# DeltaNet with soft mixture of experts: expert weights loaded as half rows, with the ReLU restoring column order

## The chip, the cores and the metric

The kernel runs on one core of one Trainium2 chip. The metric is the device time of the whole program in microseconds. Before the change it is 296.39 us, the median of three runs (295.6 to 298.61).

## The reference

First comes a delta-rule attention over 768 steps, for 4 batches and 8 heads of 48 dimensions. Its output, as 3072 rows of 384 columns, is the input x of a soft mixture of 8 experts with 4 slots each.

```python
for t in range(S):                                  # S = 768
    y[:, :, t] = einsum('bhd,bhde->bhe', q[:, :, t], state)
    v_old = einsum('bhde,bhd->bhe', state, kt)      # kt is the normalised key
    state = state + bt * einsum('bhd,bhe->bhde', kt, vt - v_old)

logits = x @ phi                                    # 3072 x 32
d = softmax(logits, over the rows);  slot_input = d.T @ x
for e in range(8):
    h = maximum(slot_input[e] @ w1[e], 0.0)         # w1[e] is 384 x 1024
    slot_out[e] = h @ w2[e]                         # w2[e] is 1024 x 384
out = softmax(logits, over the slots) @ slot_out    # 3072 x 384
```

All is float32. Each w1 and w2 is 12.6 MB over the eight experts.

## The kernel before

The recurrence is cut into 12 chunks of 64 steps. For each chunk the kernel loads k, q and v (`load`, `load_q`; rows of 192 bytes), transposes them, forms the Gram matrices, inverts a triangular system (`invert`, `join`), and steps the state (`step`). As chunks finish, `route` and `pair` transpose the outputs, compute logits and accumulate the slot inputs. The mixture's tail then runs: a merge of partial sums, `first` (slot inputs times w1, ReLU, transposes), `second` (times w2), and the combination with its stores.

All work is recorded as operations of a `Plan`. Three tables written into the file fix everything afterwards: `ORDER` gives the order in which the operations are issued, `PLACE` the address of each buffer, and `ALTS` which engine takes an operation that several could do. So a loop in the source does not tell the order on an engine. Waits between engines and transfers are put in where the regions that two instructions touch overlap. SyncE (SP) and GpSimd (POOL) issue the weight loads, each among its other work. A transfer that SP issues also waits for the one eight places before it.

Weights. A w1 tile holds, for expert e and kk in 0..2, one row of 1024 columns on each of 128 partitions (partition p has row 3p + kk). It is loaded by two transfers: columns 0 to 511 into the first half of the tile, 512 to 1023 into the second. There are 24 such tiles, so 48 transfers of 256 KB: 32 issued by SP, 16 by POOL (L1029). A w2 tile holds, for expert e and tp in 0..3, two rows of 384 columns on each partition (t = 2 tp and 2 tp + 1). Each row is one transfer into its half of the tile. There are 32 such tiles, so 64 transfers of 192 KB: 46 by SP, 18 by POOL (L1040).

`first(qq)` takes four experts at a time (a quartet), side by side in the four row groups of one PSUM bank. For each half f of the hidden columns it accumulates three products per expert (L1090), then a ReLU with the expert's mask evicts the bank into the half f of `hr` (L1099, on ScalarE). Eight transposes (L1106) read `hr` with a stride of 8, so that they need both halves, and give `hT`. The order table runs the second quartet's products first.

`second` (L1123) runs twice, for the halves h of the 384 output columns. It loops over both quartets and over tp; each (quartet, tp) is a group of 8 matmuls: t even for four experts, then t odd for four experts. The columns that a matmul reads in a w2 tile start at `x = Dm * (t % 2) + HD * h`, with Dm = 384 and HD = 192. After each pass a copy (L1128), a product that sums the experts' rows (L1129) and a scaling (L1130) give the slots' outputs; the combination (L1142) and the stores follow (L1150: 48 transfers of 96 KB on SP, POOL and ScalarE). Matmuls in float32 stand as two instructions each in the profile.

Of the kernel before, what the change touches and what calls it, by code (L numbers as in the profile page):

```python
# [11 lines left out]
ALU = mybir.AluOpType  # L12
ACT = mybir.ActivationFunctionType
# [183 lines left out]
def kernel(  # L197
# [11 lines left out]
    nc = tc.nc  # L209
# [5 lines left out]
    E, Dm, F = moe_w1.shape  # L215
# [14 lines left out]
    def A(b, n=None):  # L230
        if b.psum:
            return pb[:, b.addr:b.addr + b.size, :]
        return sb[:, b.addr:b.addr + (n or b.size)]
# [40 lines left out]
    ENG = {"SP": nc.sync, "ACT": nc.scalar, "POOL": nc.gpsimd, "DVE": nc.vector}  # L274
# [11 lines left out]
    V = nc.vector  # L286
# [718 lines left out]
    for n in range(N):  # L1005
# [7 lines left out]
        for m in ([n - 1] if n else []) + ([n] if n == N - 1 else []):  # L1013
            route(m)
            if m % 2:
                pair(m // 2)

    w1b, w2b = {}, {}
    done = qslot + [kslot[x % NK] for x in (N - 1, *range(N - NK, N - 2))]
    last = [kslot[(N - 2) % NK]]  # L1020
    for e in range(E):
        for kk in range(NKT):
            w1b[e, kk] = t = done.pop(0) if done else pl.buf(F)
            pl.tag = ("w1", e)

            def go(q, e=e, kk=kk, t=t):
                s = moe_w1[e].rearrange("(p k) f -> p k f", k=NKT)
                for x in H2:
                    ENG[q].dma_start(out=A(t)[:, 512 * x:512 * x + 512], in_=s[:, kk, 512 * x:512 * x + 512])  # L1029
            pl.soft = [chain[8]]  # L1030
            pl.op(dq(0.8, 1.2, None), None, go, w=[t], bus=1.5, nd=2)
    for e in range(E):
        for tp in range(NFC // 2):
            w2b[e, tp] = t = last.pop() if last and e == E - 1 else pl.buf(2 * Dm)
            pl.tag = ("w2", e)

            def go(q, e=e, tp=tp, t=t):
                s = moe_w2[e].rearrange("(p t) d -> p t d", t=NFC)
                for x in H2:
                    ENG[q].dma_start(out=A(t)[:, Dm * x:Dm * x + Dm], in_=s[:, 2 * tp + x])  # L1040
            pl.soft = [chain[N - 1]]
            pl.op(dq(0.8, 1.2, None), None, go, w=[t], bus=1.15, nd=2)
    pl.soft = []
# [34 lines left out]
    HF = F // 2  # L1078

    def first(qq):  # L1080
        pl.tag = ("first", qq)
        hr = pl.buf(F)
        hTb[qq] = pl.buf(F)
        for f in H2:
            ph = pl.buf(1, psum=True)

            def prod(f=f, ph=ph):
                for kk in range(NKT):
                    for j in range(4):
                        mm(A(ph)[32 * j:32 * j + 32, 0], A(slb)[:, NSL * kk:NSL * kk + NSL],  # L1090
                           A(w1b[4 * qq + j, kk])[:, f * HF:f * HF + HF], start=kk == 0)
            pl.op("PE", 2.6, prod, r=[slb] + [w1b[4 * qq + j, kk] for j in range(4) for kk in range(NKT)], w=[ph], rec=24, act=3072)

            def relu(e, f=f, ph=ph):
                o = A(hr)[:, f * HF:f * HF + HF]
                if e == "DVE":
                    V.tensor_scalar(o, A(ph)[:, 0], 0.0, XMSK(qq), op0=ALU.max, op1=ALU.mult)
                else:
                    nc.scalar.activation(o, A(ph)[:, 0], ACT.Relu, scale=XMSK(qq))  # L1099
            pl.op([("ACT", 0.69), ("DVE", 0.75)], None, relu, r=[ph, cxm], w=[(hr, f)])  # L1100
        for t4 in H2:
            pt = pl.buf(1, psum=True)

            def turn4(t4=t4, pt=pt):
                for i in range(4):
                    nc.tensor.transpose(A(pt)[:, 0, P * i:P * i + P], A(hr)[:, 4 * t4 + i::NFC], ident())  # L1106
            pl.op("PE", 0.5, turn4, r=[hr, cident], w=[pt], rec=4, act=512)
            pl.op(ev(512), None, lambda e, t4=t4, pt=pt: copy(
                e, A(hTb[qq])[:, 512 * t4:512 * t4 + 512], A(pt)[:, 0]), r=[pt], w=[(hTb[qq], t4)])

    first(0)
    first(1)
    HD = Dm // 2
    for h in H2:
        pl.tag = ("second", h)
        pso = pl.buf(1, psum=True)
        for qq in H2:
            for tp in range(NFC // 2):
                def prod(tp=tp, qq=qq, h=h, pso=pso):
                    for t in (2 * tp, 2 * tp + 1):  # L1120
                        for j in range(4):
                            x = Dm * (t % 2) + HD * h
                            mm(A(pso)[32 * j:32 * j + 32, 0, 0:HD],  # L1123
                               A(hTb[qq])[:, P * t + 32 * j:P * t + 32 * j + 32],
                               A(w2b[4 * qq + j, tp])[:, x:x + HD], start=qq == 0 and t == 0)
                pl.op("PE", 0.76, prod, r=[(hTb[qq], tp // 2)] + [w2b[4 * qq + j, tp] for j in range(4)], w=[pso], rec=16, act=768)
        sj, so, p4 = pl.buf(HD), pl.buf(HD), pl.buf(1, psum=True)
        pl.op("ACT", t_act(HD), lambda sj=sj, pso=pso: nc.scalar.copy(A(sj), A(pso)[:, 0, 0:HD]), r=[pso], w=[sj])  # L1128
        pl.op("PE", 0.33, lambda p4=p4, sj=sj: mm(A(p4)[:, 0, 0:HD], A(csel4), A(sj)), r=[csel4, sj], w=[p4], rec=2, act=384)  # L1129
        pl.op("DVE", t_dvp(HD) + 0.05, lambda so=so, p4=p4: V.tensor_scalar(  # L1130
            A(so), A(p4)[:, 0, 0:HD], A(rd), None, op0=ALU.mult), r=[p4, rd], w=[so])
        pl.tag = ("out", h)
        for g2 in range(NG // 2):
            for z in H2:
                po, ob = pl.buf(2, psum=True), pl.buf(2 * Dm)

                def comb(po=po, z=z, g2=g2, so=so):
                    for x in H2:
                        for b in H2:
                            p0 = 32 * (2 * z + b)  # L1140
                            g = 2 * g2 + x
                            mm(A(po)[:, b, HD * x:HD * x + HD], A(cT)[p0:p0 + 32, P * g:P * g + P], A(so)[p0:p0 + 32])  # L1142
                pl.op("PE", 0.72, comb, r=[(cT, 2 * g2), (cT, 2 * g2 + 1), so], w=[po], rec=8, hold=[ob], act=384)
                pl.op(ev(2 * Dm), None, lambda e, po=po, ob=ob: copy(
                    e, A(ob).rearrange("p (b f) -> p b f", b=2), A(po)[:, :, 0:Dm]), r=[po], w=[ob])
                for b in H2:
                    def put(e, ob=ob, z=z, b=b, g2=g2, h=h):
                        o = out.rearrange("(y b g s t) d -> y b s t g d", y=2, b=2, g=NG, s=2)
                        for y in H2:
                            ENG[e].dma_start(out=o[y, b, z][:, 2 * g2:2 * g2 + 2, HD * h:HD * h + HD],  # L1150
                                             in_=A(ob)[ha(y), Dm * b:Dm * b + Dm].rearrange("p (x d) -> p x d", x=2))
                    pl.op(dq(0.85, 1.45, 0.95), None, put, r=[ob], bus=0.7, nd=2)
# [29 lines left out]
```

## Time and profile before

| what | value |
|---|---|
| median of the runs | 296.39 us |
| the profiled execution: time, span | 296.42 us, 294.7 us |
| granted TensorE clock, mean | 0.938 |
| TensorE busy (PE) | 228.9 us, 78% of the span |
| VectorE, ScalarE, GpSimd busy | 197.6, 145.2, 140.2 us |
| bytes moved | 45.13 MB, mean 153 GB/s |
| packets | 81519 in all, 74704 of them under 2 KB |

The span runs from the first to the last instruction; the profiled execution's own time has 1.7 us around it. PE is a TensorE matmul, PEld its weight load, DVE is VectorE, ACT is ScalarE. L12 is line 12 of the kernel before. A row of a group names line, engine, operation, output and input, count, busy time with the mean of one in ns, and the idle time before it with what ended it. A row of the windows has, for a stretch, the busy time and count of PE, PEld, DVE, ACT and POOL, then the granted clock, the busy share of the 16 DMA engines and GB/s. A row of transfers names the issuing queue (SPq is SP's), the count, the size of one and the median time from issue to landing; a row of a DMA queue has packets, MB and its share of the 16 engines (q1 carries what SP issues, q0 what POOL issues).

### The profile page before, as it was taken

Reading aid. Unit: us, or ns where it says so; the run is one execution under the profiler, and the core shown is the slowest. Engines: PE = TensorE matmul, PEld = TensorE weight load, DVE = VectorE, ACT = ScalarE, POOL = GpSimd, SP = SyncE. Lnnn points to the kernel's source line nnn. Section 1 sums busy time; section 2 is a strip of 40 time slices with the busy share of each in tenths; the row PEclk is TensorE's granted clock in tenths of the full one; section 3 lists DMA queues with packets and bytes.
Section 4 is the critical chain, followed back from the end, with each engine's and each line's share of the span. In section 5 each row is a group of like instructions: output and inputs, shape, how many; then the busy total and the mean of one; then the engine's idle time right before and its main releaser. Section 6 shows DMA issues by size and latency. Waiting matters only on the chain.

```text
span 294.7 us, 14440 instructions
## 1 busy us (share of the span) xinstructions
PE 228.9 (78%) x6252; PEld 186.2 (63%) x6252; DVE 197.6 (67%) x504; ACT 145.2 (49%) x325; POOL 140.2 (48%) x225
## 2 busy tenths in 40 slices
PE   0784778982988897798979877787866988999950
PEld 0663677872887786686868775766654864366640
DVE  3468979989866689777699889883773667213130
ACT  1253487774828466668736768562311532230321
POOL 8997569454493364226762545641640320200460
PEclk9997599999579999999899999999997999999985
DMA  8979642453431361336545407785696599990887
GB/s 147 162 155 166 111 79 56 97 107 56 87 56 34 73 118 33 62 54 136 116 94 118 153 4 232 215 190 177 200 349 218 178 349 375 349 364 13 213 226 206
DMA packets 81519, 45.13 MB, mean 153 GB/s; under 512 B 63520, under 2 KB 74704, under 8 KB 81456
## 3 DMA queue, kind: packets, MB, share of 16 engines
q1 hardware_dynamic: 72704, 30.28, 42.3%
q0 software_dynamic: 5232, 12.56, 15.0%
q10 hardware_dynamic: 3520, 1.38, 2.0%
q8 instruction: 49, 0.80, 1.1%
q14 instruction: 14, 0.11, 0.1%
HBM read 39.47 MB, written 4.72 MB: 150 GB/s over the span
## 4 chain that ended last, share of the span: by engine, by line
PE 27%; DVE 12%; issue 8%; SPq 4%; ACT 4%; POOL 2%; DMA 1%; DVEq 0%; POOLq 0%; ACTq 0%
SPq L1150 4%; DVE sb L277 4%; PE pb L1090 4%; PE pb L716 3%; PE pb L821 3%; ACT sb L281 2%; PE pb L1123 2%; PE pb L782 2%; PE pb L902 2%; PE pb L791 2%; POOL sb L277 2%; PE pb L504 2%; PE pb L867 1%; PE pb L920 1%; PE pb L953 1%
## 5 line engine op out<-in xcount | busy, mean ns | idle before, releaser
L281 ACT ACTIVATE sb<-pb 128x512 f32<-128x512 f32 (+5 forms) x144 | 76.0, 559 | 91.2 <-PE pb L473 22.9
L277 POOL TENSOR_TENSOR sb<-sb 128x256 f32<-128x256 f32 (+10 forms) x89 | 64.7, 735 | 66.8 <-DVE sb L277 33.5
L277 DVE TENSOR_TENSOR sb<-sb 128x126 f32<-128x126 f32 (+10 forms) x153 | 52.9, 347 | 11.2 <-POOL sb L277 6.7
L283 DVE COPY sb<-pb 128x512 f32<-128x512 f32 (+5 forms) x43 | 26.2, 617 | 27.3 <-PE pb L473 5.9
L473 PE MATMUL pb<-sb 128*128 128x128 f32 x192 | 32.7, 318 | 15.0 <-DMA sb<-in_q_dram 9.6
L473 PEld LDWEIGHTS pb<-sb 128*128 128x128 f32 x192 | 24.7, 161 | 19.4 <-issue 11.7
L716 PE MATMUL pb<-sb 64*64 64x32 f32 x1152 | 27.3, 231 | 11.9 <-DVE sb L277 4.7
L716 PEld LDWEIGHTS pb<-sb 64*64 64x64 f32 x1152 | 25.0, 147 | 15.2 <-issue 7.3
L504 PE MATMUL pb<-sb 64*64 64x128 f32 x768 | 28.2, 287 | 5.8 <-ACT sb L281 4.2
L840 PE MATMUL pb<-sb 64*64 64x48 f32 x768 | 26.2, 220 | 3.9 <-DVE sb L770 1.9
L840 PEld LDWEIGHTS pb<-sb 64*64 64x64 f32 x768 | 24.2, 135 | 6.6 <-DVE sb L770 2.5
L504 PEld LDWEIGHTS pb<-sb 64*64 64x64 f32 x768 | 22.7, 140 | 9.0 <-ACT sb L281 5.4
L782 PE MATMUL pb<-sb 64*64 64x48 f32 x768 | 26.0, 220 | 2.3 <-issue 2.3
L782 PEld LDWEIGHTS pb<-sb 64*64 64x64 f32 x768 | 24.1, 135 | 2.7 <-issue 2.5
L1040 POOL DMA_DIRECT2D sb<-in_moe_w_dram x18 | 9.7, 543 | 32.9 <-PE pb L953 16.1
L821 PE MATMUL pb<-sb 128*64 128x96 f32 x352 | 19.2, 260 | 3.2 <-ACT sb L281 1.6
L791 PE MATMUL pb<-sb 128*64 128x96 f32 x352 | 18.9, 261 | 1.9 <-ACT sb L513 0.8
L412 POOL DMA_DIRECT2D sb<-in_k_dram x35 | 19.7, 570 | 0.7 <-DVE sb L341 0.7
L821 PEld LDWEIGHTS pb<-sb 128*64 128x64 f32 x352 | 16.8, 145 | 4.9 <-ACT sb L281 2.2
L1150 POOL DMA_DIRECT2D out_dram<-sb x14 | 8.4, 607 | 23.8 <-DVE sb L283 18.5
L513 ACT ACTIVATE sb<-pb,sb 128x128 f32<-128x128 f32 x48 | 16.9, 368 | 4.9 <-PE pb L504 4.7
L791 PEld LDWEIGHTS pb<-sb 128*64 128x64 f32 x352 | 16.4, 145 | 3.6 <-issue 1.5
(142 smaller groups left out, 376.4 us busy)
## 6 DMA issues: line engine op xcount, KB each, us to landing
sb<-in_moe_w_dram SPq DMA_DIRECT2D x46, 192.0 KB, 5.5
sb<-in_moe_w_dram SPq DMA_DIRECT2D x32, 256.0 KB, 4.0
sb<-in_moe_w_dram POOLq DMA_DIRECT2D x16, 256.0 KB, 5.3
sb<-in_moe_w_dram POOLq DMA_DIRECT2D x18, 192.0 KB, 6.1
sb<-in_q_dram SPq DMA_DIRECT2D x14, 192.0 KB, 4.4
out_dram<-sb SPq DMA_DIRECT2D x24, 96.0 KB, 3.5
sb<-in_v_dram SPq DMA_DIRECT2D x22, 96.0 KB, 3.3
sb<-in_v_dram SPq DMA_DIRECT2D x88, 24.0 KB, 2.8
```

The costliest lines, as they stand in the source:

```text
L277: ENG[e].tensor_tensor(*a, **kw)
L281: nc.scalar.activation(o, i, ACT.Copy)
L283: V.tensor_copy(o, i)
L412: ENG[e].dma_start(out=d()[p0:p0 + w, x], in_=s[t0:t0 + w, hs])
L473: nc.tensor.transpose(A(ps)[:, 0, P * j:P * j + P], A(src)[:, x:x + P], ident())
L504: mm(A(ps)[ha(r), c, P * j4:P * j4 + P].rearrange("p (a t) -> p a t", a=2), x[ha(c), j, r, 0], x[ha(c), j, r])
L716: mm(A(ps)[ha(b), x, 64 * j:64 * j + RW].rearrange("p (a t) -> p a t", t=w), st, m)
L782: mm(pv(pY)[ha(1 - r), j // 4, j % 4, c], A(at)[ha(r), 512 * c + 64 * j:512 * c + 64 * j + 64], hv(u)[ha(r), j, c], start=first and c == 0 ...
L791: mm(A(pY)[ha(1 - r), j // 4, 96 * (j % 4):96 * (j % 4) + 96], kqv(KQ[n])[:, j, r, 1], Sv(n)[:, j, r], start=j % 4 == 0)
L821: mm(A(pR)[ha(r), j // 4, 96 * (j % 4):96 * (j % 4) + 96], kqv(KQ[n])[:, j, r, 0], Sv(n)[:, j, r])
L840: mm(pv(pW)[ha(r), j // 4, j % 4, c], A(zs)[ha(r), 64 * (zj * c + z0 + j):64 * (zj * c + z0 + j) + 64], hv(R)[ha(r), j, c])
L1150: ENG[e].dma_start(out=o[y, b, z][:, 2 * g2:2 * g2 + 2, HD * h:HD * h + HD], in_=A(ob)[ha(y), Dm * b:Dm * b + Dm].rearrange("p (x d) -> p ...
```

## The change

Each w1 transfer now takes, from every row, columns 256x to 256x + 255 and 512 + 256x to 512 + 256x + 255, for x = 0 or 1: two pieces of 1 KB in place of one of 2 KB. They fill half x of the tile. Each w2 transfer takes columns 192x to 192x + 191 of both rows t: two pieces of 768 B in place of one of 1536 B, again into half x of the tile.

`first` still reads half f of a w1 tile, but its 512 results are now hidden columns 256f and up and 512 + 256f and up, so that the ReLU writes them as two blocks of 256 that lie 512 apart and `hr` has the old order again. `second` reads its columns from `x = Dm * h + HD * (t % 2)`: pass h reads half h of each tile alone. The order of instructions on every engine, their number apart from a wait, the issuing queues and the buffers stay as they were.

```diff
--- before.py
+++ after.py
@@ -1015,6 +1015,7 @@
             if m % 2:
                 pair(m // 2)
 
+    HD = Dm // 2
     w1b, w2b = {}, {}
     done = qslot + [kslot[x % NK] for x in (N - 1, *range(N - NK, N - 2))]
     last = [kslot[(N - 2) % NK]]
@@ -1026,7 +1027,8 @@
             def go(q, e=e, kk=kk, t=t):
                 s = moe_w1[e].rearrange("(p k) f -> p k f", k=NKT)
                 for x in H2:
-                    ENG[q].dma_start(out=A(t)[:, 512 * x:512 * x + 512], in_=s[:, kk, 512 * x:512 * x + 512])
+                    ENG[q].dma_start(out=A(t)[:, 512 * x:512 * x + 512].rearrange("p (a f) -> p a f", a=2),
+                                     in_=s[:, kk].rearrange("p (a b f) -> p b a f", a=2, b=2)[:, x])
             pl.soft = [chain[8]]
             pl.op(dq(0.8, 1.2, None), None, go, w=[t], bus=1.5, nd=2)
     for e in range(E):
@@ -1037,7 +1039,8 @@
             def go(q, e=e, tp=tp, t=t):
                 s = moe_w2[e].rearrange("(p t) d -> p t d", t=NFC)
                 for x in H2:
-                    ENG[q].dma_start(out=A(t)[:, Dm * x:Dm * x + Dm], in_=s[:, 2 * tp + x])
+                    ENG[q].dma_start(out=A(t)[:, Dm * x:Dm * x + Dm].rearrange("p (t f) -> p t f", t=2),
+                                     in_=s[:, 2 * tp:2 * tp + 2, HD * x:HD * x + HD])
             pl.soft = [chain[N - 1]]
             pl.op(dq(0.8, 1.2, None), None, go, w=[t], bus=1.15, nd=2)
     pl.soft = []
@@ -1092,11 +1095,12 @@
             pl.op("PE", 2.6, prod, r=[slb] + [w1b[4 * qq + j, kk] for j in range(4) for kk in range(NKT)], w=[ph], rec=24, act=3072)
 
             def relu(e, f=f, ph=ph):
-                o = A(hr)[:, f * HF:f * HF + HF]
+                o = A(hr).rearrange("p (a b f) -> p b a f", a=2, b=2)[:, f]
+                i = A(ph)[:, 0].rearrange("p (a f) -> p a f", a=2)
                 if e == "DVE":
-                    V.tensor_scalar(o, A(ph)[:, 0], 0.0, XMSK(qq), op0=ALU.max, op1=ALU.mult)
+                    V.tensor_scalar(o, i, 0.0, XMSK(qq), op0=ALU.max, op1=ALU.mult)
                 else:
-                    nc.scalar.activation(o, A(ph)[:, 0], ACT.Relu, scale=XMSK(qq))
+                    nc.scalar.activation(o, i, ACT.Relu, scale=XMSK(qq))
             pl.op([("ACT", 0.69), ("DVE", 0.75)], None, relu, r=[ph, cxm], w=[(hr, f)])
         for t4 in H2:
             pt = pl.buf(1, psum=True)
@@ -1110,7 +1114,6 @@
 
     first(0)
     first(1)
-    HD = Dm // 2
     for h in H2:
         pl.tag = ("second", h)
         pso = pl.buf(1, psum=True)
@@ -1119,7 +1122,7 @@
                 def prod(tp=tp, qq=qq, h=h, pso=pso):
                     for t in (2 * tp, 2 * tp + 1):
                         for j in range(4):
-                            x = Dm * (t % 2) + HD * h
+                            x = Dm * h + HD * (t % 2)
                             mm(A(pso)[32 * j:32 * j + 32, 0, 0:HD],
                                A(hTb[qq])[:, P * t + 32 * j:P * t + 32 * j + 32],
                                A(w2b[4 * qq + j, tp])[:, x:x + HD], start=qq == 0 and t == 0)
```

## The prediction

> **What bounds the kernel now.** I read the page first (engines, slices, queues), then the chain of waits, then the last 60 us by windows, waits and timeline, because all that the change touches, the two weight loads, runs from 133 us on.
>
> ```profile
> span 294.7 us, 14440 instructions
> PE   228.9 (78%) x6252; PEld 186.2 (63%) x6252; DVE 197.6 (67%) x504; ACT 145.2 (49%) x325; POOL 140.2 (48%) x225
> DMA  8979642453431361336545407785696599990887
> q1 hardware_dynamic: 72704, 30.28, 42.3%
> q0 software_dynamic: 5232, 12.56, 15.0%
> q8 instruction: 49, 0.80, 1.1%
> PE 27%; DVE 12%; issue 8%; SPq 4%; ACT 4%; POOL 2%; DMA 1%; DVEq 0%; POOLq 0%; ACTq 0%
> ```
>
> TensorE is busy for 78% of the span and holds the largest share of the chain. DMA as such has 1% of the chain, but the row of slices shows four nines in a row just before 266 us. The windows say what these are:
>
> ```profile
> 232.00:238.00 6.00, 6.00 (x232) 5.34 (x224) 3.88 (x13) 2.18 (x8) 3.18 (x6) 1.00 0.68 212
> 238.00:264.00 26.00, 23.44 (x259) 11.91 (x258) 10.90 (x43) 8.77 (x25) 3.20 (x6) 1.00 1.02 364
> 266.00:271.00 5.00, 5.00 (x106) 3.42 (x102) 0.61 (x2) 0.32 (x1) 0.00 (x0) 1.00 0.01 3
> ```
>
> The last two columns are the busy share of the DMA engines and GB/s. From 238 to 264 us the queues never run dry (1.02, 364 GB/s), from 266 to 271 us they are empty. TensorE runs through all of it:
>
> ```profile
> 249.64 10.51 PE L1090 MATMUL pb<-sb 128*32 128x512 f32 x96 [0.15 <-DVE sb L1069]
> 262.54 6.06 PE L1123 MATMUL pb<-sb 128*32 128x192 f32 x144
> ```
>
> Neither block of expert products has a long wait: both are bound by TensorE, and the weights arrive just before they are wanted. So the change lengthens a transfer stage that today is hidden, and the question is how much cover it has.
>
> **The change part by part.**
>
> *Packets.* A row of 2 KB (w1) or 1536 B (w2) becomes two of 1 KB or 768 B; the bytes stay. No load of 768 B stands in the trace, so its price is bounded from rows of other sizes.
>
> ```profile
> 5.00:8.00 3.00, 0.11 (x1) 0.14 (x2) 2.14 (x11) 0.00 (x0) 2.92 (x8) 1.00 1.32 213
> 244.00:249.00 5.00, 4.14 (x36) 2.11 (x36) 4.00 (x16) 1.69 (x9) 0.00 (x0) 1.00 1.05 376
> 285.00:290.00 5.00, 0.00 (x0) 0.00 (x0) 0.48 (x1) 0.81 (x1) 2.39 (x5) 0.55 0.99 290
> ```
>
> The first window holds loads of q and k in rows of 192 B, the second w2 loads of 1536 B, the third output stores of 768 B. With 16 engines a packet costs 16 x 192 / 213 = 14.4 ns, 16 x 1536 / 376 = 65.4 ns and 16 x 768 / 290 = 42.4 ns. A straight line through the two loads is 7.1 ns for a packet and 0.0379 ns for a byte; it gives 36.2 ns at 768 B, so a pair costs 72.5 instead of 65.4 ns (+11%), and two of 1 KB 91.8 instead of 84.7 ns (+8%). By the stores' row a pair costs 84.8 ns (+30%). The lower end is nothing: the same bytes in more packets have no reason to go faster, and the upper end is the stores' +30%. I take the line, since it rests on loads, as these are. For a transfer of 128 rows that is 128 x 7.1 / 16 = 57 ns, for w1 as for w2.
>
> The Trainium skill, "DMA: Bandwidth & Descriptors", section Specifications, states 512 B as the smallest transfer for line rate. By it both new sizes would still be at line rate and this term would be nothing (the fourth case below). The trace has its 768 B stores at 290 GB/s against 376 for the 1536 B loads, which speaks against the rule, though a store is not a load.
>
> Only SP's transfers pay it. POOL's queue already packs rows: on the page q0 has 12.56 MB in 5232 packets, 2.4 KB each, longer than a row of either weight; I count its packets as unchanged.
>
> *How late the weights get.* Transfers issued from 235 us up to the tightest one:
>
> ```profile
> sb<-in_moe_w_dram SPq DMA_DIRECT2D x29, 192.0 KB, 5.6
> sb<-in_moe_w_dram SPq DMA_DIRECT2D x4, 256.0 KB, 6.0
> L1040 SPq DMA_DIRECT2D sb<-in_moe_w_dram x1: 327/327/327, 259.0 to 259.0; - x1
> DMA to landing us min/median/max: 4.7/4.7/4.7
> ```
>
> These are 33 on SP in one backlog, so the last is late by 33 x 0.057 = 1.9 us. It is expert 2's fourth w2 tile (tp = 3), issued at 259.0 and landed 4.7 us later, at 263.8. The 144 matmuls of 6.06 us are nine groups of 0.67 us; this tile is read in the fourth, and there after two other experts: 262.54 + 3 x 0.67 + 0.1 = 264.7. Its cover is 0.9 us, so TensorE waits 1.9 - 0.9 = 1.0 us. By the lower price it waits nothing; by the stores' price the delay is 29 x 0.157 + 4 x 0.21 = 5.4 us and the wait 4.5 us. Behind the waiting matmul stand the rest of the group, the sum over experts (L1129), the first combination (L1142), its eviction and then the stores, whose issue on SP is the tail of the chain; nothing there has slack, so the wait counts in full. Later tiles gain the same 1.0 us of time, so they add nothing. The last w1 transfer has more room:
>
> ```profile
> L1029 SPq DMA_DIRECT2D sb<-in_moe_w_dram x1: 646/646/646, 249.5 to 249.5; - x1
> DMA to landing us min/median/max: 4.8/4.8/4.8
> ```
>
> It lands at 254.3. The second quartet's products run first, so it is wanted in the twelfth product of the third quarter of L1090's 10.51 us: 249.64 + 5.25 + 2.1 = 257.0. That is 2.7 us of cover, more than the 1.9 us that the whole backlog adds by 263.8.
>
> *Each transfer its own half.* The first column pass now reads the first transfer of each w2 tile alone, the second pass the other. A tile's second transfer is thus wanted some 5 us later. No wait for it exists today, so this saves nothing; it only takes the second transfers off the danger list. For w1 nothing moves: a column half already came with one transfer.
>
> *Issue.* On SP the nearest row with an extra level on 128 partitions is phi's:
>
> ```profile
> L456 SPq DMA_DIRECT2D sb<-in_moe_phi_dram x1: 432/432/432, 12.0 to 12.0; - x1
> L1040 SPq DMA_DIRECT2D sb<-in_moe_w_dram x46: 327/335/1575, 213.5 to 262.3; - x46
> L1150 SPq DMA_DIRECT2D out_dram<-sb x24: 595/626/1495, 271.8 to 291.3; - x24
> L1029 POOL DMA_DIRECT2D sb<-in_moe_w_dram x16: 536/537/603, 160.5 to 236.0; - x16
> L1150 POOL DMA_DIRECT2D out_dram<-sb x14: 602/602/641, 272.9 to 286.8; - x14
> 187.01 3.30 POOL L1029 DMA_DIRECT2D sb<-in_moe_w_dram x6 [2.04 <-ACT sb L513]
> ```
>
> SP's 0.33 us becomes 0.43 (0.6 at most). In the backlog SP issues 33 transfers in 24 us, 0.73 us apart, held by earlier transfers, so this is hidden; without that cover it would be 33 x 0.1 = 3.3 us of SP's time. POOL's issue goes from 0.54 to 0.60 at most; for its 16 transfers of w1 and 18 of w2 that is 34 x 0.06 = 2 us over 100 us, in which POOL sits idle next to these issues (2.04 us before the burst of six). Taken at nothing.
>
> *ReLU.* Four instructions now read two blocks of 256 and write them 256 apart.
>
> ```profile
> L281 ACT ACTIVATE sb<-pb 128x512 f32<-128x512 f32 x47 | 26.9, 599 | 27.2 <-PE pb L473 22.9 <-PE pb L761 2.6 <-PE pb L1106 1.3
> L543 ACT ACTIVATE sb<-pb 128x512 f32<-128x512 f32 x16 | 9.6, 603 | 3.7 <-DVE sb L528 1.9 <-PE pb L504 1.8
> L1099 ACT ACTIVATE sb<-pb,sb 128x512 f32<-128x512 f32 x4 | 2.6, 685 | 8.9 <-PE pb L1090 8.9
> ```
>
> L543 is such a rearranged copy of the same size, 603 against 599 ns. One of the four ReLUs is on the chain: 0.0 us, at most 0.1.
>
> *TensorE's instructions.* Before the backlog TensorE loses time to something that no engine releases:
>
> ```profile
> PE pb L920 <- issue: 4.1, 1, 4.1
> PE pb L782 <- issue: 2.3, 2, 1.2
> PE pb L716 <- issue: 1.9, 2, 1.1
> PE pb L821 <- issue: 0.8, 1, 0.8
> PE pb L791 <- issue: 0.8, 1, 0.8
> q0 software_dynamic: 257, 0.76, 47.1%
> q1 hardware_dynamic: 502, 0.69, 45.6%
> q8 instruction: 1, 0.02, 1.7%
> sb<-in_moe_w_dram POOLq DMA_DIRECT2D x6, 192.0 KB, 7.1
> sb<-in_moe_w_dram SPq DMA_DIRECT2D x4, 192.0 KB, 8.7
> ```
>
> The waits (177 to 226 us) add up to 9.9 us. The page's instruction queue moved 49 blocks of 16 KB, one for every 255 of the 12,504 instructions of PE and PEld. The next three rows are the queues from 219.7 to 224.0 us, around the longest wait (219.79 to 223.92): one instruction block came through, beside weights that took 93% of the engines. I read this as TensorE waiting for a block that queues behind weight transfers. If such a block waits for bytes ahead of it, SP's half of the wait grows by 11%: 9.9 x 0.5 x 0.11 = +0.5 us (+1.5 by the stores' price). If it waits for a number of packets, SP's half holds half the bytes: 9.9 x 0.5 x 0.5 = -2.5 us. I take nothing, between the two: transfers issued from 214 to 222 us take 7.1 and 8.7 us to land (the last two rows) while TensorE is back within 4.1, so a block does overtake part of the bytes.
>
> *Sum.* The profiled execution took 296.42 us (span 294.7 and 1.7 around it), the median of the runs is 296.39, the same. 296.4 + 1.0 (w2) + 0 (w1, issue, ReLU, instruction blocks) = 297.4 us. One per cent, 3.0 us, is about what a measurement of this kernel can tell from no change.
>
> **The rivals.**
>
> *Packets cost what the stores' do.* For it: the 290 GB/s row is the only one with 768 B. Against it: stores of three issuers, and the line through the loads. Place: the same w2 tile; it decides from a delay of 0.9 us on, and over 1% from about +22%. Time: 296.4 + 4.5 + 1.5 = 302.4 us, slower.
>
> *Instruction blocks get ahead.* If the engines take turns by packets, each weight packet ahead of a block is half as long. For it: the overtaking above; against it: the wait of 4.1 us is far longer than a turn of a few 84 ns packets. Time: 296.4 + 1.0 - 2.5 = 294.9 us; if POOL's half shrinks too, 292.4, which is faster by over 1%. The Trainium skill, "DMA: Bandwidth & Descriptors", section on queues, rings and completion order, says an engine alternates between rings packet by packet; the 4.1 us agrees badly with it, as a block would wait for single packets only.
>
> *Hidden anyway.* The packets cost nothing extra that the cover of 0.9 us doesn't hold (a price under +5%): 296.4 us. For it: DMA has 1% of the chain. Against it: the line through the loads.
>
> **How the numbers follow.** Forecast 297.4 us: 0.42, with its own range 296.5 to 299 (a price of +5 to +20%). Stores' price 302.4: 0.25. Instruction blocks ahead 294.9: 0.17. Hidden 296.4: 0.16. The range of 8 in 10 reaches from 294.5, below the 294.9 case but not to its lower end, to 301.5, short of the stores' full price. Faster by over 1% (below 293.4): half of the third case, 0.09. Slower by over 1% (above 299.4): the second and 0.05 of the forecast's tail, 0.30. Within 1%: 0.61.
>
> **What would show it.** In the profile of after: q1 should have some 10,000 more packets; the window 238 to 264 us about 340 GB/s at the same DMA share; SP's w2 issues to landing about 6 us; L1126 (L1123 before) a wait of about 1 us for a weight transfer in the fourth group; L1093 none; the ReLU rows 0.69 us; PE's waits named issue still near 10 us in 177 to 226. The forecast is wrong if L1126 runs through without a wait, if L1093 waits for w1, if the issue waits change by over 2 us, or if v loads, behind SP's longer issues, hold up a step.

## The result and the profile after

The changed kernel takes 300.25 us, the median of 20 runs (297.31 to 302.23), against 296.27 us for the kernel before in the 20 runs beside them. The ratio is 1.0138, with a 95% interval of 1.0105 to 1.017: slower by 1.4%. The forecast of 297.4 us was 2.85 us short; the time lies inside the range, but in the class (slower by over 1%) that had been given 0.30. A ratio compares only the runs within 1.5% of the fastest run of their own kernel, a median all of them, so one very fast run can move a ratio, and for differences of about 1% the two can say different things.

The page of the changed kernel: span, the two weight queues (packets, MB, share of 16 engines), the chain by engine, and SyncE's w2 transfers (count, size, us from issue to landing).

```profile
span 297.5 us, 14441 instructions
q1 hardware_dynamic: 82688, 30.28, 43.8%
q0 software_dynamic: 5232, 12.56, 15.6%
PE 27%; DVE 11%; issue 6%; DMA 6%; ACT 4%; SPq 3%; POOL 2%; POOLq 0%; DVEq 0%; ACTq 0%
sb<-in_moe_w_dram SPq DMA_DIRECT2D x46, 192.0 KB, 6.0
```

q1 has 9,984 more packets for the same 30.28 MB, q0 has none more. DMA's share of the chain went from 1% to 6%: weights now set a part of the end. Two windows of the same profile (the last three columns are TensorE's granted clock, the busy share of the DMA engines, and GB/s):

```profile
238.00:264.00 26.00, 23.78 (x250) 11.11 (x242) 9.56 (x40) 8.89 (x25) 4.32 (x6) 0.93 1.07 326
244.00:249.00 5.00, 3.99 (x28) 2.19 (x31) 3.77 (x18) 1.23 (x5) 0.00 (x0) 0.87 1.09 329
```

The engines are as busy as before (1.07 and 1.02) and move 326 GB/s where they moved 364. In the 5 us of w2 loads it is 329 instead of 376, so a packet of 768 B costs 16 x 768 / 329 = 37.3 ns. (Both windows also hold GpSimd's longer packets, 0.39 of 1.88 MB before and 0.24 of 1.64 MB after, so these are prices of a mixture.) The Trainium skill, "DMA: Bandwidth & Descriptors", section Specifications, puts line rate at 512 B and more; both sizes are above that, and the trace disagrees by 12%.

TensorE's timeline (start, length, count, and in brackets the idle time before with its releaser):

```profile
247.91 8.63 PE L1093 MATMUL pb<-sb 128*32 128x512 f32 x64 [0.15 <-DVE sb L1072]
262.44 2.47 PE L1126 MATMUL pb<-sb 128*32 128x192 f32 x52
266.18 4.10 PE L1126 MATMUL pb<-sb 128*32 128x192 f32 x92 [1.28 <-DMA sb<-in_moe_w_dram]
270.21 0.59 PE L1132 MATMUL pb<-sb 128*128 128x192 f32 x2
```

The 144 matmuls that took 6.06 us without a stop now stop after 52 = 3 x 16 + 4 of them, in the fourth group, which is the place the prediction named. The idle time shown is 1.28 us, but from the first matmul to the sum over experts (L1132) it takes 7.77 us instead of the 5.99 before (262.54 to 268.53 there): 1.78 us longer. That is more than the idle gap, because the gap counts from the end of the matmul before it. One of these matmuls takes 0.33 us by its own row, but 144 in a row take 6.06 us, one every 0.042 us: they overlap. The begin of the 53rd matmul says more. In the profile of before it had not begun by 264.67, 2.13 us into the pass (PE and PEld, then the clock, DMA share and GB/s), and in a window 0.02 us longer (x55) it had:

```profile
262.54:264.67 2.13, 2.13 (x52) 1.72 (x56) 1.00 1.03 361
```

After the change it begins at 266.18, 3.74 us into the pass, so it is delayed by 1.6 us. The transfer that was waited for:

```profile
L1042 SPq DMA_DIRECT2D sb<-in_moe_w_dram x1: 368/368/368, 260.8 to 260.8; - x1
  PE pb L1126: 1.3, 1
DMA to landing us min/median/max: 5.3/5.3/5.3
```

Issued at 260.8 and landed at 266.1, it is expert 2's tile tp = 3, at 263.8 before. The small costs, first all of SyncE's w2 issues (ns min/median/max), then two groups of the page's kind (us in total, mean ns), then TensorE's waits without a releaser from 177 to 226 us:

```profile
L1042 SPq DMA_DIRECT2D sb<-in_moe_w_dram x46: 367/370/1822, 213.6 to 264.5; - x46
```

```profile
L1042 POOL DMA_DIRECT2D sb<-in_moe_w_dram x18 | 13.0, 725 | 31.8 <-PE pb L953 15.3 <-PE pb L1093 12.1 <-DVE sb L283 3.5
L1103 ACT ACTIVATE sb<-pb,sb 128x512 f32<-128x512 f32 x4 | 2.8, 688 | 10.4 <-PE pb L1093 10.3
```

```profile
PE pb L920 <- issue: 4.1, 1, 4.1
PE pb L782 <- issue: 1.1, 2, 0.8
PE pb L867 <- issue: 0.7, 1, 0.7
PE pb L821 <- issue: 0.6, 1, 0.6
PE pb L716 <- issue: 0.2, 1, 0.2
PE pb L791 <- issue: 0.2, 1, 0.2
```

SyncE's issue went from 0.33 to 0.37 us, GpSimd's from 0.54 to 0.725, the ReLU from 685 to 688 ns. TensorE's waits without a releaser add up to 6.9 us. In the profile of before they are 10.6 us; the prediction's 9.9 is the sum of the five longest rows only.

So 1.8 us of the loss can be seen in one place, and the medians differ by 4.0. The experiments had to say what makes the tile late, whether both halves of the change are needed, and whether the rest goes the same way. Theory A, as the expectations call it: packets lengthen the backlog, and TensorE pays what exceeds its cover. Rivals: the clock, the order of transfers, costs elsewhere.

### The profile page after: what moved, and what is told of

The parts are those of the page before. It is cut to its first block, busy times and chain, and to the rows that moved or that the text cites. A ratio compares the mean times of both kernels' runs of the same rounds, so it can differ in the third digit from the quotient of the medians.

```text
span 297.5 us, 14441 instructions
## 1 busy us (share of the span) xinstructions
PE 232.3 (78%) x6252; PEld 187.9 (63%) x6252; DVE 197.0 (66%) x504; ACT 145.4 (49%) x325; POOL 146.5 (49%) x225
## 3 DMA queue, kind: packets, MB, share of 16 engines
q1 hardware_dynamic: 82688, 30.28, 43.8%
## 4 chain that ended last, share of the span: by engine, by line
PE 27%; DVE 11%; issue 6%; DMA 6%; ACT 4%; SPq 3%; POOL 2%; POOLq 0%; DVEq 0%; ACTq 0%
DVE sb L277 4%; DMA sb<-in_moe_w_dram 4%; PE pb L1126 3%; PE pb L791 3%; PE pb L902 2%; ACT sb L281 2%; PE pb L716 2%; PE pb L782 2%; PE pb L821 2%; SPq L1153 2%; PE pb L840 2%; PE pb L867 2%; POOL sb L277 2%; PE pb L504 2%; PE pb L1093 2%
## 5 line engine op out<-in xcount | busy, mean ns | idle before, releaser
L473 PE MATMUL pb<-sb 128*128 128x128 f32 x192 | 33.1, 320 | 14.7 <-DVE sb L329 8.0
L716 PE MATMUL pb<-sb 64*64 64x32 f32 x1152 | 26.7, 227 | 10.9 <-DVE sb L277 4.6
L716 PEld LDWEIGHTS pb<-sb 64*64 64x64 f32 x1152 | 24.3, 142 | 14.2 <-issue 5.8
L504 PE MATMUL pb<-sb 64*64 64x128 f32 x768 | 27.3, 280 | 6.0 <-ACT sb L281 4.2
L840 PE MATMUL pb<-sb 64*64 64x48 f32 x768 | 27.5, 226 | 3.0 <-DVE sb L770 1.7
L840 PEld LDWEIGHTS pb<-sb 64*64 64x64 f32 x768 | 25.6, 142 | 5.6 <-DVE sb L770 2.2
L1042 POOL DMA_DIRECT2D sb<-in_moe_w_dram x18 | 13.0, 725 | 31.8 <-PE pb L953 15.3
L782 PE MATMUL pb<-sb 64*64 64x48 f32 x768 | 27.3, 226 | 1.3 <-issue 1.1
L504 PEld LDWEIGHTS pb<-sb 64*64 64x64 f32 x768 | 22.0, 136 | 9.2 <-ACT sb L281 5.4
L782 PEld LDWEIGHTS pb<-sb 64*64 64x64 f32 x768 | 25.5, 142 | 1.7 <-issue 1.6
L821 PE MATMUL pb<-sb 128*64 128x96 f32 x352 | 19.2, 260 | 3.4 <-ACT sb L281 1.8
L791 PE MATMUL pb<-sb 128*64 128x96 f32 x352 | 19.8, 271 | 1.7 <-DVE sb L827 0.9
L412 POOL DMA_DIRECT2D sb<-in_k_dram x35 | 19.7, 570 | 0.7 <-DVE sb L341 0.7
L821 PEld LDWEIGHTS pb<-sb 128*64 128x64 f32 x352 | 16.7, 145 | 5.2 <-ACT sb L281 2.4
L791 PEld LDWEIGHTS pb<-sb 128*64 128x64 f32 x352 | 17.4, 153 | 3.4 <-DVE sb L827 1.0
```

The source lines that it names most:

```text
L412: ENG[e].dma_start(out=d()[p0:p0 + w, x], in_=s[t0:t0 + w, hs])
L473: nc.tensor.transpose(A(ps)[:, 0, P * j:P * j + P], A(src)[:, x:x + P], ident())
L504: mm(A(ps)[ha(r), c, P * j4:P * j4 + P].rearrange("p (a t) -> p a t", a=2), x[ha(c), j, r, 0], x[ha(c), j, r])
L716: mm(A(ps)[ha(b), x, 64 * j:64 * j + RW].rearrange("p (a t) -> p a t", t=w), st, m)
L782: mm(pv(pY)[ha(1 - r), j // 4, j % 4, c], A(at)[ha(r), 512 * c + 64 * j:512 * c + 64 * j + 64], hv(u)[ha(r), j, c], start=first and c == 0 ...
L791: mm(A(pY)[ha(1 - r), j // 4, 96 * (j % 4):96 * (j % 4) + 96], kqv(KQ[n])[:, j, r, 1], Sv(n)[:, j, r], start=j % 4 == 0)
```

## The experiments

### The change again, and each half of it

after_again is the changed kernel once more. w1_only keeps w2 as before, w2_only keeps w1 and the ReLU as before:

```diff
 w1_only: L1029, L1030 (1 KB pieces) and the ReLU of the change; w2 loads and
          x = Dm * (t % 2) + HD * h as before
 w2_only: L1040 (768 B pieces, a half of the columns each) and
          x = Dm * h + HD * (t % 2) of the change; w1 loads and ReLU as before
```

> The changed kernel once more, for a second profile. Late weights (theory A: packets cost 14% more in the backlog of 238 to 266 us, the second expert product waits for a w2 tile, and that wait goes to the end): ratio 1.010 to 1.017, a wait of 1 to 1.6 us in the rows of L1126 for a weight transfer, and the store stage as long as before. Clock (theory B: what is over the wait comes from stretches at half TensorE clock that the changed kernel draws more often): mean granted clock near 0.92 again, two or more half-clock stretches of 3.4 us after 200 us, against one in the profile of before.

> w1 in pieces of 1 KB with the rearranged ReLU, w2 as before in 1536 B rows. Theory A: only 4 of the 33 transfers of SP in the last backlog get longer, 0.06 us each, under the cover of 0.9 us: no wait over 0.5 us in L1123's place, ratio 1.000 to 1.004. If the cost lies in w1's packets, in GpSimd's longer issue of w1 or in the ReLU: ratio 1.007 or more.

> w2 in pieces of 768 B, each transfer in its own half, w1 and ReLU as before. Theory A: 29 of the 33 transfers get longer, wait in the second product 0.8 to 1.4 us, ratio 1.007 to 1.014, most of the changed kernel's. If the cost lies with w1: ratio 1.000 to 1.004.

Measured, against 296.9 us for the kernel before in 18 runs: after_again 299.71 us, ratio 1.0175 (1.0076 to 1.0273); w1_only 297.42 us, 1.0112 (1.0041 to 1.0182); w2_only 297.21 us, 1.0082 (1.0038 to 1.0126). after_again on the timeline, and behind it the landing of the same tile:

```profile
250.14 6.22 PE L1093 MATMUL pb<-sb 128*32 128x512 f32 x56 [0.15 <-DVE sb L1072]
263.10 2.77 PE L1126 MATMUL pb<-sb 128*32 128x192 f32 x52
267.37 4.10 PE L1126 MATMUL pb<-sb 128*32 128x192 f32 x92 [1.50 <-DMA sb<-in_moe_w_dram]
```

```profile
L1042 SPq DMA_DIRECT2D sb<-in_moe_w_dram x1: 368/368/368, 262.6 to 262.6; - x1
DMA to landing us min/median/max: 4.7/4.7/4.7
```

The wait stands at the same matmul again. Neither half alone has it; the first column pass takes the old 6.06 us in w1_only and, below it, in w2_only:

```profile
262.22 6.06 PE L1125 MATMUL pb<-sb 128*32 128x192 f32 x144
```

```profile
262.50 6.06 PE L1124 MATMUL pb<-sb 128*32 128x192 f32 x144
```

That does not yet show that both halves are needed. TensorE's clock over the first products, from 246 to 262.5 us, was not the same in the four profiled executions (after, after_again, w1_only, w2_only in this order, a fence each; the third column from the right is the clock):

```profile
246.00:262.50 16.50, 15.92 (x126) 6.57 (x130) 4.72 (x20) 4.06 (x9) 2.88 (x4) 0.90 1.06 319
```

```profile
246.00:262.50 16.50, 15.42 (x132) 6.72 (x132) 5.70 (x26) 4.18 (x10) 2.88 (x4) 1.00 1.07 328
```

```profile
246.00:262.50 16.50, 16.17 (x130) 6.90 (x134) 4.76 (x20) 4.18 (x10) 2.13 (x4) 0.90 1.05 367
```

```profile
246.00:262.50 16.50, 16.46 (x119) 6.08 (x119) 3.75 (x16) 3.35 (x8) 2.88 (x4) 0.80 1.06 327
```

From the first product (L1093) to the first of the second layer it took 13.0 us at a clock of 1.00, 14.5 at 0.90 and 15.8 at 0.80. A slow stretch there gives the weights 1.5 to 2.9 us more, so the halves' executions had cover that before's own (12.9 us) had not. The measure that this does not touch is the landing of the tightest tile counted from the first product's start:

| kernel | first product | tile lands | difference | later than before |
|---|---|---|---|---|
| before | 249.64 | 263.76 | 14.1 | |
| w1_only | 247.81 | 262.5 | 14.7 | 0.6 |
| w2_only | 246.74 | 262.8 | 16.1 | 2.0 |
| after | 247.91 | 266.1 | 18.2 | 4.1 |
| after_again | 250.14 | 267.3 | 17.2 | 3.1 |
| after_third (below) | 251.21 | 268.5 | 17.3 | 3.2 |

So w2's pieces carry most of the lateness, w1's four transfers in the backlog little, and the whole change somewhat more than the sum of the two, 3.1 to 4.1 against 2.6 us. At full clock w2_only would have wanted the tile at 246.74 + 12.9 + 2.1 = 261.8 and had it at 262.8, an estimated wait of 1.1 us (its expectation had 0.8 to 1.4); w1_only would have wanted it at 262.9 and had it at 262.5.

The times of the halves do not decide between the expectations. By its ratio w1_only lies where its expectation saw a cost in w1 itself (1.007 or more), far above the 1.000 to 1.004 of theory A. By the medians w1_only is 0.5 us above before and w2_only 0.3 us, so that neither has a cost clear of noise. The landings speak for theory A, the ratio of w1_only against it.

That a changed kernel is granted a slower clock is not seen: the mean granted clock was 0.924 in after_again's runs and 0.9225 in those of before beside them, and 0.915 and 0.919 for after_third (below).

### The second halves held back

late_halves is the changed kernel in which SyncE issues the second transfer of a w2 tile only six tiles later (all of the first pass's data ahead of it); w2_late is the same on w2_only.

```diff
+    held, seen, LATE = [], [], 6
...
+                one(0)                                   # columns of the first pass
+                held.append(partial(one, 1))             # columns of the second pass
+                seen.append(1)
+                while len(held) > (LATE if len(seen) < 23 else 0):
+                    held.pop(0)()
```

> The changed kernel, but SP holds back the second transfer of each w2 tile (read by the second pass alone) until six more tiles' first transfers are out; the last ones go out together. Theory A: the tiles that the first pass reads land 2 to 3 us earlier, no wait for a transfer in L1126 over 0.3 us, and the time falls by the wait: ratio to before 1.000 to 1.006. Theory B, or a cost before the tail: the wait is gone and the ratio stays at 1.009 or more.

> w2 in packets of 768 B, each transfer in its own half, and SyncE holding back the second transfers by six tiles, as in late_halves; w1 and ReLU as before. Theory A (the backlog grows by packets, only the first transfers are wanted early): no wait for weights in either layer's products, and the second pass to the first store takes 9.2 to 9.7 us as in before; ratio 1.000 to 1.008, not above w2_only's 1.008. Rival D (holding transfers back costs as much as it saves, since SyncE then issues two transfers in a row and the last second halves come late): a wait of 0.5 to 1.5 us in the second column pass of the second layer, ratio over 1.01.

late_halves: no wait for weights, though its first pass takes 6.50 us; but 300.43 us, ratio 1.01 (0.9972 to 1.0228). w2_late: no wait either, the pass takes 6.06 us, ratio 0.9972 (0.9933 to 1.0012), while its median is 299.97 against 298.38. Holding back takes the wait away, as theory A says of a tile that is wanted early. Whether it gives the time back is not settled. late_halves did not come down to the 1.000 to 1.006 that theory A expected, and its median is 3.5 us above before; by its ratio w2_late is no slower than before, by its median 1.6 us slower.

### The dose: no cut, and quarters

whole_rows loads each tile of the old layout in one transfer of uncut rows; quarter_rows cuts the rows into four, with ReLU and products adapted.

```diff
 whole_rows:
-                for x in H2:
-                    ENG[q].dma_start(out=A(t)[:, Dm * x:Dm * x + Dm], in_=s[:, 2 * tp + x])
+                ENG[q].dma_start(out=A(t)[:, 0:2 * Dm].rearrange("p (t f) -> p t f", t=2), in_=s[:, 2 * tp:2 * tp + 2])
 quarter_rows:
+                s = moe_w2[e].rearrange("(p t) (c x f) -> p x (t c) f", t=NFC, c=2, x=2)
+                    ENG[q].dma_start(out=A(t)[:, Dm * x:Dm * x + Dm].rearrange("p (u f) -> p u f", u=4),
+                                     in_=s[:, x, 4 * tp:4 * tp + 4])
```

> The layout of before, but each tile comes in one transfer whose rows are not cut at all: 4 KB a packet for w1, 3 KB for w2, so half the packets of before. Theory A (packets lengthen the backlog from 238 to 266 us, and TensorE pays only what exceeds its cover): the line through the loads gives 123.5 ns for 3072 B in place of 2 x 65.4, so the backlog ends some 1.5 to 2 us earlier than before, nothing waits in the second layer's products, and as before has no wait there to lose, the time is that of before: ratio 0.997 to 1.003. Theory C (each packet also costs TensorE time outside the backlog, since the two halves of the change, each without a wait for weights, were still 0.8 and 1.1% above before): ratio 0.990 to 0.995, and the first expert products start about 1 us earlier. A tile is complete only as a whole, so w1's first column half could come later: a wait at the first products speaks for neither.

> Twice the dose: rows cut into quarters, 512 B a packet for w1 and 384 B for w2; still two transfers a tile, each in its own half. For w2 both transfers of a tile are read by the first pass, as in before. Theory A: by the line of 7.1 ns a packet a transfer of 128 rows becomes 0.17 us longer than in before, so the 33 transfers of the backlog end 5.6 us later; the wait in the second layer's products is 4.5 to 6 us and the time 302 to 304 us, ratio 1.018 to 1.028. Rival D (the 1.3 to 1.5 us of wait in the changed kernel come from the order of transfers, or from something that both halves of the change must meet, and not from the price of a packet): the wait stays at 0 to 2 us and the ratio under 1.016. Under the line packets of 384 B still run at 16 x 384 / 21.7 = 283 GB/s; if these small rows cost more than the line, the wait is over 7 us.

Measured against 298.38 us (31 runs): whole_rows 299.26 us, ratio 0.9952 (0.991 to 0.9994); quarter_rows 305.73 us, 1.0232 (1.0193 to 1.0272). The window 244 to 249 us of whole_rows, then of quarter_rows:

```profile
244.00:249.00 5.00, 4.05 (x32) 2.52 (x36) 3.81 (x18) 1.23 (x5) 0.00 (x0) 1.00 1.03 399
```

```profile
244.00:249.00 5.00, 4.13 (x52) 1.66 (x42) 3.61 (x15) 1.81 (x9) 0.00 (x0) 1.00 1.12 319
```

3072 B at 399 GB/s are 123 ns a packet, where the prediction's line gives 123.5; 384 B at 319 are 19.3 ns, where it gives 21.7. The line through two loads thus held within 11% over a factor of eight in size (GpSimd's longer packets are in all these windows). quarter_rows on the timeline, and the later of its tightest tile's two transfers, both of which the 53rd matmul reads here:

```profile
250.71 5.51 PE L1092 MATMUL pb<-sb 128*32 128x512 f32 x36
265.44 1.27 PE L1125 MATMUL pb<-sb 128*32 128x192 f32 x22
267.17 0.86 PE L1125 MATMUL pb<-sb 128*32 128x192 f32 x16 [0.46 <-DMA sb<-in_moe_w_dram]
268.42 0.85 PE L1125 MATMUL pb<-sb 128*32 128x192 f32 x14 [0.39 <-DMA sb<-in_moe_w_dram]
271.12 4.19 PE L1125 MATMUL pb<-sb 128*32 128x192 f32 x92 [1.85 <-DMA sb<-in_moe_w_dram]
```

```profile
L1041 SPq DMA_DIRECT2D sb<-in_moe_w_dram x1: 487/487/487, 267.2 to 267.2; - x1
  PE pb L1125: 1.9, 1
DMA to landing us min/median/max: 3.8/3.8/3.8
```

It lands at 271.0. The tile's first transfer, with which the table can be compared, was issued at 266.6 and landed at 270.4, 19.7 us after the first product: 5.6 us late, as 33 x 0.17 says. That the number is met so well is in part luck: more than 33 transfers were in the queue, and an added packet cost less here than with half rows (both below, where the lateness is taken apart). The waits are 2.7 us, below the expected 4.5 to 6, since a slow stretch in the first products gave 1.8 us (14.7 in place of 12.9). The pass up to the sum takes 9.80 us, 3.8 more than before. Where half rows add one packet to a row, quarters add three; the lateness, the pass's loss and the excess in the ratio (2.3% against 1.4%) all grow, by less than threefold. Rival D, with 2 us of wait and 1.016 at most, falls. The medians differ by 7.4 us, of which the pass shows half.

whole_rows brings half a per cent by the ratio and loses 0.9 us by the medians. Its ratio lies between the ranges of theories A and C, and its first products start 1.8 us before those of before, as C expected; but without any such edit they start between 246.7 and 251.3 us in these profiles. So theory C, a small cost of packets outside the backlog, is not excluded.

### The same backlog, made lighter

light_before and light_after are the two kernels without six of the w2 loads (of 32 tiles; the expectation's 64 is the number of transfers).

```diff
+    INSTEAD = {(7, 0): 4, (3, 0): 1, (7, 1): 5, (1, 1): 2, (0, 3): 1, (6, 2): 7}
...
+                if (e, tp) in INSTEAD:
+                    return
...
-                               A(w2b[4 * qq + j, tp])[:, x:x + HD], start=qq == 0 and t == 0)
+                               A(w2b[INSTEAD.get((4 * qq + j, tp), 4 * qq + j), tp])[:, x:x + HD], start=qq == 0 and t == 0)
```

> The kernel before, leaving out the loads of six of the 64 w2 tiles (twelve of SyncE's transfers, 2.4 MB of the backlog); the products that would read them read another expert's tile of the same group instead, so the work on TensorE is the same. With them gone the backlog ends some 6 us earlier. Both theories: nothing waited in the second layer's products before, so the second pass to the first store stays at 9.25 us and the ratio is 0.995 to 1.0.

> The changed kernel with the same six tiles left out in the same way. Theory A (all that the change costs goes through the backlog's end): the tightest tile now lands some 5 us before it is wanted, no wait, second pass to first store 9.25 to 9.5 us, and the time is that of light_before within 0.3% (ratio to before 0.993 to 1.003). Rival G (the smaller packets also cost 1 to 2 us elsewhere: the ReLU, GpSimd's longer issues, blocks of TensorE's instructions, weights that land late in earlier steps): no wait here either, but 1 to 2 us over light_before, ratio to before 1.000 to 1.005 or more.

> The changed kernel once more, on the chip of light_before and light_after, so that the three differences can be set against each other. Theory A: ratio to before 1.010 to 1.018, a wait of 1.0 to 2.0 us for a weight transfer in the fourth group of the second layer's products, 11 to 11.6 us from the second pass to the first store.

Measured beside 298.61 us for the kernel before (29 runs): light_before 298.54 us, ratio 1.0002 (0.9963 to 1.0041); light_after 298.26 us, 1.001 (0.9961 to 1.0058); after_third 301.64 us, 1.0116 (1.006 to 1.0172). The second layer's first pass on the timelines of light_before, light_after and after_third, and the tile of after_third:

```profile
263.12 6.06 PE L1126 MATMUL pb<-sb 128*32 128x192 f32 x144
```

```profile
265.77 6.06 PE L1129 MATMUL pb<-sb 128*32 128x192 f32 x144
```

```profile
251.21 5.00 PE L1093 MATMUL pb<-sb 128*32 128x512 f32 x32
265.53 2.47 PE L1126 MATMUL pb<-sb 128*32 128x192 f32 x52
268.53 4.10 PE L1126 MATMUL pb<-sb 128*32 128x192 f32 x92 [0.53 <-DMA sb<-in_moe_w_dram]
```

```profile
L1042 SPq DMA_DIRECT2D sb<-in_moe_w_dram x1: 368/368/368, 261.9 to 261.9; - x1
DMA to landing us min/median/max: 6.6/6.6/6.6
```

With twelve of SyncE's transfers gone, all the small pieces, the longer issues and the rearranged ReLU are still there, and the change costs nothing that can be measured: the two light kernels differ by 0.3 us in the median, the full ones by 3.0 on the same chip. light_after's last weight transfer lands at 260.2 + 5.2 = 265.4 us, before its first pass begins. So at least the larger part of what the change costs goes through the backlog's end. The intervals leave room for about 0.5%, or 1.5 us, elsewhere, so that rival G's 1 to 2 us is not ruled out at its lower end. That light_before is no faster than before says again that before had no wait there.

### TensorE's instruction waits

fewer_queued is the kernel before with four w2 tiles of GpSimd (eight transfers issued from 211 to 216 us) given to SyncE after 228 us; whole_fewer adds it to whole_rows.

```diff
 ORDER: ops 1057, 1054, 1043, 1058 moved to stand behind op 1037
 ALTS:  these four from "1" (POOL) to "0" (SP)
```

> The kernel before, with four of the w2 tiles (eight transfers) that GpSimd issues from 211 to 216 us issued by SyncE from about 228 us on, where the DMA engines stand idle between two bursts. Theory E (TensorE's longest wait without a releaser, 4.1 us at L920 from 219.8 to 223.9, is for a block of its instructions that queues behind weight transfers): with 1.57 MB less in the queues at that time the wait falls to 2.5 us or less, and the waits named issue from 177 to 250 us from 11.0 to 9 or less. Rival F (this wait is not tied to the load on the queues): 4.1 us as before. The eight transfers go to the backlog's start, so its end may come later: if the backlog starts at 228 it still ends by 266 and nothing waits in the second layer's products (ratio 0.99 to 1.0); if the idle gap is not used, a wait of up to 3 us there (ratio 1.005 to 1.01).

> whole_rows and fewer_queued in one: uncut rows in one transfer a tile, and four of GpSimd's w2 tiles moved to SyncE after 228 us. Both were slightly faster than before by the comparison (0.995 and 0.994) and by different means. Theory A with E: the moved tiles lengthen the backlog, the uncut rows shorten it by about as much, so no wait in the second layer's products; the instruction waits from 177 to 250 us are 9 us or less against 11.0; ratio 0.985 to 0.995. Rival H (both gains are scatter between executions): ratio 0.995 to 1.003.

fewer_queued: 298.18 us, ratio 0.9935 (0.9895 to 0.9976). whole_fewer: 296.94 us beside 298.61, ratio 0.9942 (0.9902 to 0.9981). TensorE's waits named issue: in fewer_queued at the line that was L920, then in whole_fewer at this line and at the one with the longest wait.

```profile
PE pb L923 <- issue: 1.1, 1, 1.1
```

```profile
PE pb L843 <- issue: 4.2, 3, 3.1
...
PE pb L923 <- issue: 1.2, 1, 1.2
```

In the profiled executions of before, the changed kernel (three), w1_only, w2_only, late_halves and both light kernels this wait is 3.9 to 5.0 us, in quarter_rows 3.6, in whole_rows 2.3 and in w2_late 2.0; with the eight transfers gone it is 1.1 and 1.2. So the traces bear out theory E, that this wait hangs on what is queued beside it, though not on those eight transfers alone. That TensorE waits for instructions there is a reading: the profile names no releaser. The Trainium skill, "Runtime: NRT & Kernel Launch", section Instruction fetch mechanics, says that the engine fetches its next 256 instructions by a DMA queue of its own and that this is mostly hidden; if that is what these waits are, it is not hidden here, with single waits of up to 5.0 us. But the total is not tied to it: from 177 to 250 us it was 7.6 us in fewer_queued, 7.1 in after without any such edit, and 12.6 in whole_fewer, where 9 or less was expected. So what made fewer_queued and whole_fewer faster is open. whole_fewer is the one version whose median and ratio are both better than before's on its chip by 0.6% (fewer_queued has the ratio, but only 0.2 us in the median); its added value over fewer_queued alone is not shown.

## Why the prediction was right and wrong

**The place and the mechanism** held in all three profiles of the changed kernel: loads in smaller packets, a backlog from 238 us that TensorE hides only just, and a stop at one tile in the fourth group. The first products had no wait for w1, the later tiles none, and SyncE alone had more packets.

**The price of a packet** nearly held: 37.3 ns at 768 B against the line's 36.2 and the stores' 42.4 (a pair is +14%, not +11% or +30%). The rival with the stores' price gave 302.4 us, 2.15 us from the measured time where the forecast is 2.85 off; still its reason is refuted by the loads' own row, so that its closeness is luck. The rival by which the packets are hidden is out as well, and so is, with it, the time that the 512 B rule would give.

**The step that failed is how late the weights get.** The prediction had 33 x 0.057 = 1.9 us. Measured from the first product it is 3.1, 3.2 and 4.1 us, on average 3.5. Three things make up the missing 1.6 us, as an estimate. The price explains 0.6: a row costs 74.7 - 65.4 = 9.3 ns more instead of 7.1, so 33 transfers are 2.5 us late. The count explains 0.5: the prediction counted transfers issued from 235 us, but the queues last ran dry at 233.6 us and still held earlier ones. The rows are before's idle stretch (the last two columns, DMA share and GB/s), then SyncE's queue from its end to the landing of the tile, in before (233.6 to 263.76) and in after (232.1 to 266.14):

```profile
231.90:233.60 1.70, 1.70 (x81) 1.12 (x76) 1.21 (x3) 1.27 (x6) 0.77 (x2) 1.00 0.00 0
q1 hardware_dynamic: 5627, 7.96, 76.4%
q1 hardware_dynamic: 10978, 8.20, 79.8%
```

That is 5,351 packets more, and 5,118 and 5,212 in the other two profiles, where 33 transfers of 128 rows would add 4,224; 5,200 x 9.3 / 16 = 3.0 us. And 0.08 to 0.24 MB more went ahead of the tile than in before (8.20 against 7.96 in after), which at 320 GB/s is 0.25 to 0.75 us. In quarter_rows the same stretch took 5.3 us more for 14,700 more packets, 5.8 ns each: one price per added packet does not hold for halves and quarters alike.

**The cover** of 0.9 us held at full clock: before's 53rd matmul begins at 264.7 and its tile is there at 263.76. With 3.5 us of lateness this gives a delay of 2.6 us when TensorE runs the first products at full clock (12.9 us) and 1.1 when a slow stretch makes them 14.4. The profiled executions fit: the 53rd matmul is delayed by 2.1 us at full clock, by 1.6 and 0.9 with a stretch. The prediction had one number for cover where it differs by 1.5 us from one execution to the next.

**What a wait costs.** The prediction let the wait count in full, and it does. The pass to the sum is 1.8, 2.3 and 1.0 us longer (after, after_again, after_third) for delays of 1.6, 2.1 and 0.9 us. Only the idle gaps of the timelines, 1.28, 1.50 and 0.53 us, are smaller, as they count from the end of a matmul that overlaps the next.

**Sum.** With these sizes: 296.3 + 1.0 to 2.3 for the pass = 297.3 to 298.6 us; the medians differ by 2.8 to 4.0. The rest, 0.5 to 2.2 us, has no stage of its own. In the profile of after the span is 2.8 us longer than before: 1.7 less up to the first product, 1.6 more in the first products, 1.8 more in the pass and 1.1 more behind it. In the other two profiles the part behind the pass is 0.1 and 0.3 us longer. The light kernels say that most of the loss goes through the backlog; that executions with a faster TensorE, and so a longer wait, were more frequent than the three profiled ones, is argued and not shown.

**The small terms.** SyncE's issue, 0.37 us, was put at 0.43 and at 0.6 at most. GpSimd's, 0.725 us, broke the bound of 0.60, but its cover held, as light_after shows within its interval. The ReLU cost 3 ns. The instruction blocks were taken at nothing between +0.5 and -2.5 us. From 177 to 226 us their waits were 6.9, 7.9 and 11.0 us in three profiles of the changed kernel and 10.3 in light_after, against 10.6 in before and 8.3 in light_before. A change of over 2 us was named as a sign that the forecast is wrong, and two of three profiles show one; but versions with and without small packets overlap, so it may be scatter. The rival's time, 294.9 us, did not come. A gain in these waits, hidden by the larger loss, is neither shown nor ruled out.

## What to carry to other kernels

A stage of loads that runs full until just before its use can have next to no share of the chain to show (DMA had 1% here) and yet be one microsecond from being the bound. Take the landing of its tightest transfer, subtract it from the moment of need, and multiply the price per packet by all that is queued ahead of it since the queues last ran dry; then give the cover a spread, since it moves with the clock of the engine that consumes. To see whether the whole cost goes that way, lighten the stage in both versions and see whether their difference vanishes.

## What the runs showed of the hardware

- Loads of 384, 768, 1536 and 3072 B a packet ran at 319, 329, 376 and 399 GB/s in the same window, beside GpSimd's longer packets; the gain from longer packets does not end at 512 B here.
- GpSimd's issue of a w2 transfer took 0.54 us for one piece a row, 0.725 for two and 0.753 for four (quarter_rows, mean of 18): the step is from one to two. SyncE's went from 0.33 to 0.37 us.
- A stop of TensorE in a row of overlapping matmuls (0.33 us each, one begun every 0.042 us) cost 0.5 to 0.8 us above the idle time that the profile shows, but only 0.2 us above the delay of the matmul that waited.
- The same first products took 12.9 to 15.8 us, by the clock granted from 246 to 262.5 us (1.00 to 0.80).
